# VectorE takes the QK of one head group in turn with softmax and PV of the group before; TensorE sums QK products of four groups

## The chip, the cores and the metric

The kernel runs on one core of a Trainium2 chip. The engines named here are TensorE (PE, its weight loads PEld), VectorE (DVE), ScalarE (ACT), GpSimd (POOL) and SyncE (SP), whose queue issues almost all transfers. The metric is the device time in microseconds (us) of one execution. Kernels are compared by the median over several executions; a profile describes one execution.

## The reference

Input x has 2048 rows of 1024 numbers in bfloat16. Two layers follow, each made of two residual blocks A and B with the same weights in both layers.

```python
def A(x, wqkv, wo):                     # 32 heads of 32, window 8, dilation 2
    q, k, v = split(x @ wqkv)
    idx = pos[:, None] - 2 * arange(8)  # row p sees p, p-2, ... p-14
    mask = idx >= 0
    logits = einsum("bhsd,bhswd->bhsw", q, k[idx]) * 32 ** -0.5
    logits = where(mask, logits, -1e9)
    attn = softmax(logits)
    return einsum("bhsw,bhswd->bhsd", attn, v[idx]) @ wo

def B(x, w1, b1, w2, b2):               # mixes over the rows
    u = gelu(einsum("bsd,sf->bdf", layernorm(x), w1) + b1)
    return transpose(einsum("bdf,fs->bds", u, w2) + b2)

for _ in range(2):
    x = x + A(layernorm(x))
    x = x + B(layernorm(x))
```

## The kernel before

Since the dilation is 2, even and odd rows never meet in A. The kernel calls them the two classes (c = 0 and 1). Within a class, a partition holds J = 8 consecutive rows, so that the window of 8 is reached by slot offsets along the free dimension; the 7 slots ahead of a partition's own rows are copied from the partition before by two transfers (L272 and L273, the shift of k and v). A class has four head groups of eight heads (256 columns), so a layer's attention walks through NCH = 8 chunks, called groups 0 to 7 here: 0 to 3 are class 0, 4 to 7 are class 1.

For one group, `proj` makes q, k or v: per unit 16 matmuls of 256 columns, and one eviction by ScalarE. q, k and v have two buffers each, used alternately by group. `qk` multiplies q with shifted k for two window positions at once (L282, 4096 columns into T4) and folds the 32 products per head to 4 by three halving additions (L283 to L285), four times. `softmax_front` does the last two foldings, adds the mask, takes the maximum by three halving steps and subtracts it; ScalarE takes the exponential. `softmax_back` sums, inverts and normalises into Pb. `pv` multiplies v with Pb (L315). For the groups in `pe_pv` (0 to 3 of layer 0) TensorE adds the eight products up with an identity matrix as weights, and ScalarE copies the sums to o_q; for all others VectorE adds (L340, L343, L344). T4 is the work tile of both `qk` and `pv`. o_q, one buffer, is then transposed by a transfer into oT (L348).

After attention of a class, `out_proj` applies wo, adds the residual, stores the result and normalises it into h2, with statistics on ScalarE for class 0 (`stats_act`) and on VectorE for class 1. `gemm1` is the first product of B. Its sum over the rows needs both classes; for ten of the 14 blocks of w1 the class 0 half is computed ahead (`partials`). `gemm2_tile` is the second product, one tile of 128 rows at a time.

The order is that of the program text, which a planner turns into one in-order instruction stream per engine: it takes the instructions whose inputs are ready, those that stand earlier in the text first. `weave` makes that text: it walks through the units of `stream` (the attention), each with a cost for TensorE and one for VectorE, and whenever TensorE's sum is behind it puts in units of a filler. The filler is first `second_class` (in layer 0 the prologue of class 1, in layer 1 `gemm2_tile` for class 1 of the layer before), then `out_proj` of class 0 and `partials`. The stream's "second" puts in all that is left of the first filler; "out" changes to the next.

In `stream`, the QK units of group ci are followed by units of the projections of group ci+1; after the first QK unit comes `softmax_back` of group ci-1, after the second its whole `pv`. In layer 1 (`split`), softmax and PV of group 3 are done before "second" and before any projection of class 1.

Small tiles of 128x1024 (xr, xn, xs, xo, hb, junk, tmp) share the pool x2 with five buffers.

## Time and profile before

| what | value |
|---|---|
| median of 4 runs | 1376.67 us (1374.45 to 1377.76) |
| profiled execution | 1380.81 us, span 1379.0 us |
| mean granted TensorE clock | 0.979 |
| attention stage of layer 0 | to about 371 us |
| attention stage of layer 1 | about 624 to 1039 us |
| QK products L282 (64 of 4096 columns) | 146.4 us busy |
| PV products L315 (48 of 4096, 32 of 2048 columns) | 148.1 us busy |
| QK foldings L283, L284, L285 | 78.2, 44.1, 27.1 us busy |
| PV additions L340, L343, L344 | 14.7, 44.1, 44.1 us busy |

The span reaches from the first to the last instruction of the profiled execution; 1.8 us of its time lie around it. A line of a group of instructions names the source line, the engine, the operation, what it writes and reads by the program's names, the shape and the count; then the busy time, the mean duration of one in ns, and the idle time of the engine just before them with what ended it. A line of the timeline has the start, the duration, the engine and the group, and in brackets the idle time before it with its releaser. Matmuls overlap, so a mean of 379 ns for a 512-column matmul is a latency; the rate is read from a run of many.

### The profile page before, as it was taken

What the parts mean: (1) busy time and instruction counts of PE and PEld (TensorE: products, weight loads), DVE (VectorE), ACT (ScalarE), POOL (GpSimd) and SP (SyncE); (2) the same over time, 40 slices, a digit from 0 to 9 for tenths busy, and PEclk for the clock granted to TensorE, in tenths of its full rate; (3) what the DMA queues carried; (4) which work ended last, traced back from release to release, by engine and by line L of the source; (5) the groups of instructions that cost most, each with busy time, mean ns of one, the idle gap of its engine ahead of it and who ended that gap; (6) DMA issues with size and microseconds to landing.
All of it is one profiled execution on the core that took longest, in us unless ns stands there. A gap on an engine that the chain in (4) does not pass through costs nothing.

```text
span 1379.0 us, 17728 instructions
## 1 busy us (share of the span) xinstructions
PE 1286.8 (93%) x7328; PEld 742.8 (54%) x7328; DVE 811.1 (59%) x920; ACT 426.5 (31%) x868; POOL 10.5 (1%) x20
## 2 busy tenths in 40 slices
PE   4799889999899999999999979998998999999998
PEld 3677665664344444448866339865443444444443
DVE  4679999999750342233999975966997023211111
ACT  4852228633121341002233433664321234100000
POOL 3000000000000000000000000000000000000000
PEclk9899999999999999999999989999999999999999
DMA  9963334634362326883477883436226322243531
GB/s 221 199 149 89 81 88 135 180 106 106 92 175 61 92 67 174 226 218 87 117 175 188 213 208 102 130 108 151 77 77 180 102 78 69 82 129 101 152 100 58
DMA packets 297985, 177.22 MB, mean 129 GB/s; under 512 B 74704, under 2 KB 275408, under 8 KB 297904
## 3 DMA queue, kind: packets, MB, share of 16 engines
q1 hardware_dynamic: 297792, 176.08, 48.8%
q8 instruction: 57, 0.93, 0.3%
q0 software_dynamic: 112, 0.01, 0.1%
q14 instruction: 24, 0.20, 0.0%
HBM read 127.94 MB, written 16.78 MB: 105 GB/s over the span
## 4 chain that ended last, share of the span: by engine, by line
PE 50%; DVE 37%; DMA 5%; ACT 4%; issue 2%; SPq 1%; DVEq 0%; ACTq 0%
PE psg L476 11%; PE pso L476 11%; PE psg L454 8%; DVE T L282 8%; DVE T L315 7%; PE ps L267 5%; PE pso L454 5%; DVE T L283 4%; PE pso L421 4%; PE ps L454 3%; DVE T L343 3%; DVE o_q L344 3%; DVE T L284 2%; DMA oT<-o_q 2%; DVE St L285 1%
## 5 line engine op out<-in xcount | busy, mean ns | idle before, releaser
L267 PE MATMUL ps<-wq,hT 128*128 128x256 bf16 x3072 | 360.3, 278 | 48.7 <-DMA wq<-in_A_wqkv_dram 27.9
L267 PEld LDWEIGHTS <-hT 128*128 128x128 bf16 x3072 | 325.8, 122 | 88.0 <-issue 28.7
L476 PEld LDWEIGHTS <-w 128*128 128x128 bf16 x1792 | 175.0, 98 | 214.1 <-DMA w<-in_B_w_dram 5.6
L454 PEld LDWEIGHTS <-w 128*128 128x128 bf16 x1792 | 175.3, 98 | 209.7 <-issue 0.8
L454 PE MATMUL psg<-h,w 128*128 128x512 bf16 x896 | 209.9, 379 | 0.2 <-DVE h L216 0.2
L476 PE MATMUL pso<-g,w 128*128 128x512 bf16 x896 | 199.7, 379 | 3.8 <-DMA w<-in_B_w_dram 3.8
L476 PE MATMUL psg<-g,w 128*128 128x512 bf16 x896 | 198.9, 379 | 0.0
L282 DVE TENSOR_TENSOR T<-q,k 128x4096 bf16<-128x4096 bf16 x64 | 146.4, 2288 | 75.3 <-ACT q L269 48.8
L315 DVE TENSOR_TENSOR T<-v,Pb 128x4096 bf16<-128x4096 bf16 (+1 forms) x80 | 148.1, 1864 | 13.0 <-PE psg L330 11.3
L454 PE MATMUL pso<-h,w 128*128 128x512 bf16 x640 | 151.4, 379 | 0.6 <-ACT h L221 0.6
L421 PE MATMUL pso<-wo,oT 128*128 128x512 bf16 x512 | 122.7, 391 | 23.9 <-DMA oT<-o_q 23.2
L465 DVE TENSOR_TENSOR tmp<-pso,g 128x512 f32<-128x512 f32 x40 | 27.7, 692 | 138.0 <-PE pso L454 138.0
L421 PEld LDWEIGHTS <-oT 128*128 128x128 bf16 x512 | 51.0, 100 | 89.3 <-DMA oT<-o_q 24.9
L481 DVE SCALAR_TENSOR_TENSOR xo<-pso,b_sb,xs 128x512 bf16<-128x512 f32 x32 | 23.9, 747 | 119.6 <-PE pso L476 90.2
L481 DVE SCALAR_TENSOR_TENSOR xo<-psg,b_sb,xs 128x512 bf16<-128x512 f32 x32 | 24.0, 750 | 114.5 <-PE psg L476 114.5
L466 ACT ACTIVATE g<-tmp,b_sb 128x512 bf16<-128x512 f32 x80 | 57.7, 722 | 82.1 <-DVE tmp L465 82.1
L283 DVE TENSOR_TENSOR T<-T 128x2048 bf16<-128x2048 bf16 x64 | 78.2, 1222 | 1.2
L269 ACT ACTIVATE v<-ps 128x512 bf16<-128x512 f32 x64 | 37.1, 598 | 96.8 <-DVE T L315 49.0
L181 ACT ACTIVATE ln<-mv,eps 128x1 f32<-128x1 f32 x32 | 9.4, 294 | 179.5 <-DVE mv L190 179.5
L454 PE MATMUL ps<-h,w 128*128 128x512 bf16 x256 | 58.7, 379 | 0.0
L269 ACT ACTIVATE k<-ps 128x512 bf16<-128x512 f32 x64 | 37.5, 592 | 68.2 <-PE ps L267 62.0
L269 ACT ACTIVATE q<-ps 128x512 bf16<-128x512 f32 x64 | 37.8, 592 | 54.7 <-PE ps L267 54.6
(76 smaller groups left out, 752.2 us busy)
## 6 DMA issues: line engine op xcount, KB each, us to landing
w<-in_B_w_dram SPq DMA_DIRECT2D x96, 448.0 KB, 5.0
w<-in_B_w_dram SPq DMA_DIRECT2D x56, 512.0 KB, 4.9
wq<-in_A_wqkv_dram SPq DMA_DIRECT2D x48, 512.0 KB, 4.9
wo<-in_A_wo_dram SPq DMA_DIRECT2D x64, 128.0 KB, 2.9
xa<-xn SPq DMA_DIRECT2D x32, 256.0 KB, 2.1
xs<-xa SPq DMA_DIRECT2D x32, 256.0 KB, 4.7
k<-k SPq DMA_DIRECT2D x16, 392.0 KB, 5.5
v<-v SPq DMA_DIRECT2D x16, 392.0 KB, 5.6
```

The lines of the kernel that those rows point to most:

```text
L267: nc.tensor.matmul(ps[:, jj, :], lhsT=self.lhs(c, kt, j), rhs=wts[part][:, kt, :], start=(kt == 0), stop=(kt == KD - 1))
L269: nc.scalar.activation(out=buf[:, off + 2 * jp:off + 2 * jp + 2, :].rearrange("p j (d h) -> p j d h", h=HQ), in_=ps[:].rearrange("p j (h d ...
L282: nc.vector.tensor_tensor(out=flat, in0=qb, in1=windows(k, u0, WB, [(1, J * QW)]), op=ALU.mult)
L283: nc.vector.tensor_tensor(out=pr[:, :, 0:16, :], in0=pr[:, :, 0:16, :], in1=pr[:, :, 16:32, :], op=ALU.add)
L315: nc.vector.tensor_tensor(out=dst.rearrange("p u j (d h) -> p u j d h", h=HQ), in0=v, in1=pw, op=ALU.mult)
L343: nc.vector.tensor_tensor(out=tf[:, 0], in0=tf[:, 0], in1=tf[:, 1], op=ALU.add)
L344: nc.vector.tensor_tensor(out=of, in0=of, in1=tf[:, 0], op=ALU.add)
L421: nc.tensor.matmul(ps[:], lhsT=at_.oT[c][kt // 2][:, j, kt % 2, :], rhs=wo_t[n][kt // 4][:, kt % 4, :], start=(kt == 0), stop=(kt == KD - ...
L454: nc.tensor.matmul(ps[:], lhsT=wt[c][:, j, fl * P:(fl + 1) * P], rhs=h2[c][:, j, dc * 512:(dc + 1) * 512], start=(k == 0), stop=(k == nk - 1))
L466: nc.scalar.activation(out=gs, in_=tmp[:], func=ACT.Gelu_apprx_tanh, bias=b1_sb[:, ft:ft + 1])
L476: nc.tensor.matmul(ps[:], lhsT=w2t[ft // HF][:, ft % HF, c::DIL], rhs=g[ft // GF][:, ft % GF, dc * 512:(dc + 1) * 512], start=(ft == 0), s ...
L481: nc.vector.scalar_tensor_tensor(out=xo[:, dc * 512:(dc + 1) * 512], in0=ps[:], scalar=b2_sb[:, i, c:c + 1], in1=xs[:, dc * 512:(dc + 1) * ...
```

## The change

- The stream is arranged anew. In the stage of group ci the units of three lists are merged in proportion (`paced`): the QK operations of group ci; softmax and PV of group ci-1, one VectorE operation per unit; and the projections K and Q of group ci+1 followed by V of group ci. V is thus made one stage later than before.
- For the groups in `pe_qk` (0 to 3 of layer 0, the argument that was `pe_pv`), VectorE makes only the products for one window position at a time (2048 columns, two halves of T4 in turn), and TensorE adds eight slices of 256 columns of each with the identity matrix; ScalarE copies the sums of two positions to St.
- PV is done on VectorE, one window position at a time, with a tile of its own (Tv) and additions into o_q, for all groups but the last of each layer; that one (`pv_pe`) is done in two halves of the rows with sums on TensorE, and each half is transposed by its own transfer.
- Maximum and sum of the softmax are one reduction each. The mask is put in by a select on GpSimd, on the first partition, instead of an addition.
- In layer 1, V of group 3 is made after "second", and softmax and PV of group 3 are merged with K and Q of group 4. The unit "even" sets VectorE's sum to no less than TensorE's.
- "out" comes at group 5 in layer 0 (it came within group 4). The pool x2 has four buffers; ScalarE's statistics use h or xs as scratch, and the normalised tile is written over xs.

```diff
-    x2p = pool("x2p", 5)
+    x2p = pool("x2p", 4)
...
-    maskq = const.tile([P, W, J, HQ], BF16, name="maskq")
...
+    Tv = pers.tile([P, J, QW], BF16, name="Tv")
...
         def qk(self, ci):
             q, k = q_t[ci % 2], k_t[ci % 2]
+            if ci in self.pe_qk:
+                for u in range(0, W, WB):
+                    ps = ps_fill(u // 2)
+                    for n in range(WB):
+                        pr = T4[:, n]
+                        nc.vector.tensor_tensor(out=pr, in0=q[:], in1=k[:, u + n:u + n + J, :], op=ALU.mult)
+                        prd = pr.rearrange("p j (g e h) -> p j g (e h)", h=HQ, e=4)
+                        ng = DH // 4
+                        for gi in range(ng):
+                            nc.tensor.matmul(ps[:, n * 256:(n + 1) * 256], lhsT=ident[:], rhs=prd[:, :, gi, :],
+                                             start=(gi == 0), stop=(gi == ng - 1))
+                        if n == WB - 1:
+                            nc.scalar.copy(out=St[:, u:u + WB].rearrange("p u j e h -> p (u j e h)"), in_=ps[:])
+                        yield 0.9, 1.22
+                        yield 0.0, 0.0
+                return
...
+        def softmax(self):
+            Sv = St[:].rearrange("p u j d h -> p (u j) d h")
+            Lu = L[:].rearrange("p u x -> p x u")
             nc.vector.tensor_tensor(out=Sv[:, :, 0:2, :], in0=Sv[:, :, 0:2, :], in1=Sv[:, :, 2:4, :], op=ALU.add)
+            yield 0.0, 0.63
             nc.vector.tensor_tensor(out=L[:].rearrange("p u (j h) -> p (u j) h", h=HQ),
                                     in0=Sv[:, :, 0, :], in1=Sv[:, :, 1, :], op=ALU.add)
+            nc.gpsimd.affine_select(out=L[0:1], in_=L[0:1], compare_op=ALU.is_ge, fill=NEG, base=1 - W,
+                                    pattern=[[1, W], [1, J], [0, HQ]], channel_multiplier=0)
+            yield 0.0, 0.63
+            nc.vector.tensor_reduce(out=m2[:, 0, :], in_=Lu, axis=mybir.AxisListType.X, op=ALU.max)
+            yield 0.0, 0.63
+            nc.vector.tensor_tensor(out=L[:], in0=L[:], in1=m2[:, 0:1, :].to_broadcast([P, W, J * HQ]), op=ALU.subtract)
             nc.scalar.activation(out=L[:], in_=L[:], func=ACT.Exp, scale=scale)
+            yield 0.0, 0.63
+            nc.vector.tensor_reduce(out=m2[:, 0, :], in_=Lu, axis=mybir.AxisListType.X, op=ALU.add)
...
         def pv(self, ci):
+            for u in range(W):
+                dst = Tv if u else o_q
+                v = v_t[ci % 2][:, u:u + J, :].rearrange("p j (d h) -> p j d h", h=HQ)
+                pw = Pb[:, u].unsqueeze(2).to_broadcast([P, J, DH, HQ])
+                nc.vector.tensor_tensor(out=dst[:].rearrange("p j (d h) -> p j d h", h=HQ), in0=v, in1=pw, op=ALU.mult)
+                yield 0.0, 1.16
+                if u:
+                    nc.vector.tensor_tensor(out=o_q[:], in0=o_q[:], in1=Tv[:], op=ALU.add)
+                    yield 0.0, 1.16
+            self.transpose(ci, 0, J)
+
+        def pv_pe(self, ci):
+            hj = J // 2
+            for j0 in (0, hj):
+                accs = [ps_fill(n) for n in range(2)]
+                for u in range(W):
...
+                    nc.vector.tensor_tensor(out=t.rearrange("p j (d h) -> p j d h", h=HQ), in0=v, in1=pw, op=ALU.mult)
+                    tf = t.rearrange("p j c -> p (j c)")
+                    for n in range(2):
+                        nc.tensor.matmul(accs[n][:], lhsT=ident[:], rhs=tf[:, n * 512:(n + 1) * 512],
+                                         start=(u == 0), stop=(u == W - 1))
+                    yield 0.45, 1.3
...
+                self.transpose(ci, j0, hj)
...
+        def paced(self, *its):
+            lists = [it for it in its if it[1]]
+            total = [n for _, n in lists]
+            done = [0] * len(lists)
+            live = [iter(it) for it, _ in lists]
+            while True:
+                k = min((i for i in range(len(lists)) if live[i] is not None),
+                        key=lambda i: ((done[i] + 0.5) / total[i], i), default=None)
+                if k is None:
+                    return
+                u = next(live[k], None)
+                if u is None:
+                    live[k] = None
+                    continue
+                done[k] += 1
+                yield u
...
         def stream(self):
...
-            yield from self.proj(0, 2)
+            yield "even"
+            back = ()
             for ci in range(NCH):
+                last = ci + 1 == NCH
+                turn = self.split and not last and chunks[ci + 1][0] != chunks[ci][0]
                 if self.first and ci == 1:
                     yield "second"
+                if self.first and ci == NQ + 1:
+                    yield "out"
+                parts = [] if last or turn else [self.proj(ci + 1, 1), self.proj(ci + 1, 0)]
+                if not turn:
+                    parts.append(self.proj(ci, 2))
+                yield from self.paced((self.qk(ci), 4 * W // WB), *back, (chain(*parts), len(parts) * J // 2))
+                back = [(chain(self.softmax(), self.pv(ci)), 2 * W + 6)]
+                if turn:
+                    yield "second"
+                    yield from self.proj(ci, 2)
+                    yield from self.paced(*back, (chain(self.proj(ci + 1, 1), self.proj(ci + 1, 0)), J))
+                    back = ()
+                    yield "even"
+                    yield "out"
+            yield from self.softmax()
+            yield from self.pv_pe(NCH - 1)
...
     def gemm2_tile(c, i, w2t, src, dst, hT, on_act=False):
...
-        hb = x2("hb")
         if on_act:
-            nm, rs = stats_act(xo[:], 1.0, eps1)
-            norm_act(hb[:], xo[:], nm, rs)
+            nm, rs = stats_act(xo[:], 1.0, eps1, xs[:])
+            norm_act(xs[:], xo[:], nm, rs)
...
+            if unit == "even":
+                t[1] = max(t)
+                continue
...
                     prologue_tile(1, i, hT)
-                    yield 0.6, 0.0
+                    yield 0.0, 0.0
```

## The prediction

> **What bounds the kernel now.** I read the page's busy shares and slices first, then the timelines of TensorE and VectorE through the two attention stages, then the waits. Busy shares, the rows PE, DVE and PEclk of the slices (34.5 us each), and the chain's sum:
>
> ```profile
> PE 1286.8 (93%) x7328; PEld 742.8 (54%) x7328; DVE 811.1 (59%) x920; ACT 426.5 (31%) x868; POOL 10.5 (1%) x20
> ...
> PE   4799889999899999999999979998998999999998
> DVE  4679999999750342233999975966997023211111
> PEclk9899999999999999999999989999999999999999
> ...
> PE 50%; DVE 37%; DMA 5%; ACT 4%; issue 2%; SPq 1%; DVEq 0%; ACTq 0%
> ```
>
> VectorE is full only in two stretches, the attention of layer 0 (to about 371 us) and of layer 1 (624 to 1039); outside them TensorE is gapless. So only those stretches can move, and each ends when TensorE has done all work that may stand before the class 1 output projection. Their length is TensorE's work plus its idle time. TensorE's timeline where it stood longest (start, duration, group, idle before and its releaser):
>
> ```profile
> 42.79 13.59 PE L267 MATMUL ps<-wq,hT 128*128 128x256 bf16 x96 [6.99 <-DMA wq<-in_A_wqkv_dram]
> ...
> 371.00 26.53 PE L421 MATMUL pso<-wo,oT 128*128 128x512 bf16 x110 [6.84 <-DMA oT<-o_q]
> ...
> 690.84 5.07 PE L267 MATMUL ps<-wq,hT 128*128 128x256 bf16 x32 [4.13 <-ACT v L269]
> ...
> 824.50 1.03 PE L421 MATMUL pso<-wo,oT 128*128 128x512 bf16 x2 [7.97 <-DMA oT<-o_q]
> ...
> 921.51 5.32 PE L267 MATMUL ps<-wq,hT 128*128 128x256 bf16 x32 [2.07 <-ACT k L269]
> ...
> 1038.71 25.49 PE L421 MATMUL pso<-wo,oT 128*128 128x512 bf16 x110 [7.38 <-DMA oT<-o_q]
> ```
>
> Work at full rate: 28 matmuls of 512 columns take 6.04 us in the chain (0.216 each), 192 of 256 columns 21.12 us (0.110). Layer 0 from 42.79 to 371.00 is 328.2 us and holds 1408 projection matmuls (154.9), 128 PV sums (27.6), 144 of the class 0 output projection (31.1), 320 partial sums of the first MLP product (69.1), 18 early ones of class 1 (3.9): 286.6, so 41.6 idle or at a low clock. Layer 1 from 624.42 to 1038.71 is 414.3 us: 1536 projections (169.0), 448 of the second MLP product (96.7), 31.1, 69.1, 3.9: 369.8, idle 44.5. This 86 us is what there is to win.
>
> VectorE's timeline shows what an operation costs from start to start:
>
> ```profile
> 99.67 2.29 DVE L282 TENSOR_TENSOR T<-q,k 128x4096 bf16<-128x4096 bf16 x1 [1.11 <-PE psg L330]
> 101.99 1.23 DVE L283 TENSOR_TENSOR T<-T 128x2048 bf16<-128x2048 bf16 x1
> ...
> 109.82 2.29 DVE L282 TENSOR_TENSOR T<-q,k 128x4096 bf16<-128x4096 bf16 x1
> 112.02 0.68 DVE L292 TENSOR_TENSOR L<-St 128x512 f32<-128x512 bf16 x1
> ...
> 843.00 2.29 DVE L282 TENSOR_TENSOR T<-q,k 128x4096 bf16<-128x4096 bf16 x1 [23.56 <-ACT q L269]
> ...
> 942.16 1.23 DVE L340 TENSOR_TENSOR o_q<-T 128x2048 bf16<-128x2048 bf16 x1 [21.58 <-DMA oT<-o_q]
> ```
>
> Followed by an operation that needs its result, a product of 2.29 takes 2.32 from start to start; followed by an independent one 2.20. So a dependent neighbour adds 0.03, an independent one takes 0.09 off. The two long idles are the turn between the classes (no operation ready while K and Q of class 1 are made) and a PV that waited for its transpose.
>
> **The change, VectorE.** QK by VectorE alone is 2.288 + 1.222 + 0.689 + 0.423 = 4.62, four times 18.5 per head group. In layer 0, groups 0 to 3, it becomes eight products of 2048 columns at 1.22 (row of the PV products of that shape): 9.8, minus 8.7 each. Softmax was 0.692 + 3 x 0.688 + 0.422 + 0.287 + 0.221 before the exponential and 0.422 + 0.290 + 0.224 + 0.551 + 0.690 after: 5.86. Now 0.692 + 0.688, maximum, 0.688, sum, 0.551, 0.690. No reduction is in the trace. Nearest are 0.688 for 512 float32 and 0.422 for 256; I take 0.69, with 1.38 as upper end since it steps 256 bytes between elements. Softmax then is 4.69, minus 18.7 over 16 groups (between plus 3 and minus 27). PV on VectorE was 4 x 2.291 + 7 x 1.225 = 17.7, on TensorE 8 x 1.22 = 9.8; now 15 operations of 1.22, 18.3, for seven groups of a layer, and 16 half products of 0.69 (the 1024-column row) for the last, 11.0. Layer 0 busy: from 4 x 34.2 + 4 x 42.1 = 305 to 4 x 9.8 + 4 x 18.5 + 8 x 4.69 + 7 x 18.3 + 11.0 = 290; layer 1 from 337 to 325.
>
> Taken in turn, a group on VectorE alone has 16 QK and 22 other operations: 41.5 busy, 32 independent neighbours (minus 2.9), 6 dependent (plus 0.2): 38.8, where 290.29 to 332.07 in the trace is 41.8. A group with QK sums on TensorE: 32.8 minus 1.4 plus 0.4: 31.8, where it was 36.2 (133.87 to 170.04).
>
> The mask on GpSimd: a memset of 1x1792 takes 1.722 and of 1x56 0.134, by their slope 512 elements are 0.55; the select that makes the identity takes 0.283 for 128 columns, so 1.13 as upper end. One QK operation (0.34 to 2.3) lies between the logits and the maximum and covers it: uncovered 0 to 0.8 per group, I take 0.2, 3 us in all, the in-order VectorE queue behind it waiting too. The Trainium skill, page "SBUF — State Buffer", section "Who interferes with whom", goes against this: a Vector instruction with two SBUF inputs and a GpSimd instruction that reads SBUF block each other whole, so VectorE would stand for each select; no row here shows it, and by it the sum would hold an estimated 9 to 18 us of VectorE time instead of 3.
>
> **TensorE and the queues.** PV sums go (27.6), 256 QK sums of 256 columns come (28.2), and two last groups with PV on TensorE, 2 x 32 x 0.216 = 13.8: work plus 14. The four St evictions of such a group (about 0.6 each, like ACT's other 512-column casts) replace four casts of o_q. V of a group is now made during its own QK, not a group ahead: its buffer is then already free, which removes waits like the 4.13 at 690.84; in return PV may wait for V's shift (two copies, 5.6 us to landing), covered by the softmax and QK operations ahead (about 13 us), not in the last group, where I count 5. The weights' copies stay equal in number and only change order on SP's queue. The last transpose becomes two, each near 4.4 us; the first passes while the second half is computed, and leftover partial sums fill the rest, so the gaps of 6.84 and 7.38 go. x2 has 4 buffers for 2 tiles per step instead of 5 for 3 (on ACT) or 2: between minus 3 and plus 3, taken as 0. The scratch of the statistics, the normalised tile written over xs, the memsets of the mask and the prologue's pacing (0.6 to 0) cost nothing: ACT is 31% busy, GpSimd 10.5 us.
>
> *Layer 0.* QK of group 0 starts at 44.6 as before, that of group 1 at about 65 (K, Q and 64 sums on TensorE). Three groups of 31.8 end at 160; TensorE needs 4 x 21.1 + 28.2 + 3 (low clock at 42.79) = 116, to 159. Group 4: VectorE 38.8, TensorE 21.1, nothing else ready: 17.7 idle. From 199 TensorE has 49.3 of projections, 6.9 of sums and 100.2 of filler, VectorE 3 x 38.8 and a tail of about 25: TensorE is last. Idle: 3 + 1 + 17.7 + 2 for the clock + 5 of small waits = 29. Gain 41.6 - 29 - 7.5 = 5.
>
> On that clock: after 2.07 idle 32 matmuls took 5.32 (3.5 at full rate), after 2.00 at 308.51 none slowed. So the 17.7 in pieces of 2 us may cost 0 to 14; I take 2. The Trainium skill, page "TensorE: Matmul & The Clock Gate", section "Part 1: The HAM clock gate (the "warmup" mystery)", lets the clock fall only after an idle window of about 3.4 us, by which the same pieces would cost nothing; the 5.32 row shows it fall after less.
>
> *Layer 1.* VectorE starts at 641 as before and needs 19.4 for the first QK, three groups of 38.8 and 12 us of MLP evictions: 789. TensorE has 13.8 + 3 x 21.1 + 96.7 and 4 of weight waits: 802. V of group 3 (7.0) then fills half of the 14.5 us that the last MLP tile takes from its last matmul (811.70) to hT (826.18); idle 7.5 and 2 for the clock. PV of group 3 runs under K and Q of class 1, so the 23.56 idle on VectorE shrinks to a few. QK of group 4 starts near 833 instead of 843. After it VectorE needs 19.4 + 3 x 38.8 + 25: 994; TensorE 176 from 830: 1010. Idle left: 4 + 9.5 + 5 small = 18.5. Gain 44.5 - 18.5 - 7 = 19.
>
> Behind each stretch the class 1 output projection took 26.5 and 25.5 for 110 matmuls (23.7); leftover filler closes half of it, 2, and 0 to 6 more go by a gapless first half of layer 1; I take 3. Sum 5 + 19 + 2 + 3 = 29. The profiled execution took 1380.8 (span 1379.0 and 1.8 around it), 4.1 above the median 1376.7 of the runs; so 1352 in a profile like it, 1348 as the median.
>
> **The rivals.** *A, TensorE hides it:* the gain in VectorE is real, but idle of layer 0 stays and layer 1 gives only the turn: 8 to 12, 1366. For it: TensorE has 14 us more work and is 93% busy, and operations of two groups already alternate at places (109.82, 112.02). Against: the ends' and turn's gaps are named waits.
>
> *B, products wait for sums:* QK products use two halves of T4 and wait for TensorE, which works in order behind projection units of 1.75:
>
> ```profile
> 88.36 1.23 DVE L315 TENSOR_TENSOR T<-v,Pb 128x2048 bf16<-128x2048 bf16 x1 [1.38 <-PE psg L330]
> ```
>
> 24 products in groups 1 to 3 at 1.38 are 33 us of layer 0, and the result 1381 if all come. Against: two or three other operations stand between two products, and only 10 of 32 such products waited (11.3 in all).
>
> *C, slower:* the transposes stand late in SP's order. PV starts by writing o_q and waits for the last transpose, 21.6 at 942.16, and now QK queues behind it as well. Places are groups 5 to 7 of both layers, where residual loads share the queue. VectorE's slack (about 15 in each layer) hides most of one each; four stalls cost 86 - 30 = 56, minus 29: 1404. It decides from three.
>
> **How the numbers follow.** Forecast 0.50, A 0.25, B 0.10, C 0.15. Low: idle of only 20 and 8 left in the two stretches gives 14 + 30 + 5 = 49, 1327. High reaches past B: 1385, leaving out most of C. The forecast's own range is 1327 to 1360. A change within 0.2% (2.8 us) is about what can't be told from none; B falls there by half. Faster 0.77, same 0.04, slower 0.19.
>
> **What would show it.** Right: VectorE busy near 785; group period 38 to 39 in the second half of each layer; no idle over 3 us ahead of the class 1 output projections; VectorE idle at the turn under 10; TensorE idle near 18 in layer 0's group 4. Wrong: products of groups 1 to 3 with waits on the sums (B), o_q's first product waiting for oT (C), reductions well over 0.7, or a maximum that waits for GpSimd in each group.

## The result and the profile after

The changed kernel takes 1381.0 us as the median of 54 executions; the kernel before, on the same chips, 1376.9 us (78 executions). The ratio is 1.0028, 95% interval 1.0021 to 1.0036: slower by 0.3%. The forecast was 1348 us, so the sign is wrong and 33 us are missing. The profiled execution took 1383.15 us, span 1381.3.

The page of the changed kernel: busy time of the engines, and TensorE, VectorE and the granted clock in 40 slices of 34.5 us.

```profile
PE 1296.3 (94%) x7520; PEld 761.7 (55%) x7520; DVE 776.2 (56%) x886; ACT 424.5 (31%) x876; POOL 46.5 (3%) x28
...
PE   3799888998999999999999989998899999999998
...
DVE  4279999999550342324999929999862024211111
...
PEclk9899999999999999999999999999999999999999
```

VectorE has lost 35 us of work (811.1 to 776.2; the prediction said near 785), and GpSimd has gained 36 (10.5 to 46.5). TensorE's work by the two rates of the prediction (0.110 us for 256 columns, 0.2157 for 512) is 3072 x 0.110 + 4256 x 0.2157 = 1256 us before and 3328 x 0.110 + 4192 x 0.2157 = 1270 after: plus 14, as forecast. What the span holds beyond that work is 123 us before and 111 after. The forecast needed 80.

TensorE's timeline at seven places in the changed kernel, five of them long waits:

```profile
186.09 14.96 PE L262 MATMUL ps<-wq,hT 128*128 128x256 bf16 x112 [4.07 <-ACT k L264]
...
345.74 0.61 PE L355 MATMUL pso<-T,ident 128*128 128x512 bf16 x1 [5.09 <-DVE T L352]
...
367.77 2.54 PE L452 MATMUL pso<-wo,oT 128*128 128x512 bf16 x11
...
820.63 1.69 PE L262 MATMUL ps<-wq,hT 128*128 128x256 bf16 x7 [3.59 <-DMA hT<-xs]
...
939.34 0.59 PE L485 MATMUL pso<-h,w 128*128 128x512 bf16 x1 [5.13 <-ACT h L216]
...
993.39 0.50 PE L355 MATMUL pso<-T,ident 128*128 128x512 bf16 x1 [3.76 <-DVE T L352]
...
1014.08 2.11 PE L452 MATMUL pso<-wo,oT 128*128 128x512 bf16 x9
```

The gaps of 6.84 and 7.38 ahead of the class 1 output projection (now L452 at 367.77 and 1014.08) are gone, as forecast. In their place TensorE stands 5.09 and 3.76 us earlier, at the first PV sum of the last group, whose product VectorE has not made. Of the 320 matmuls of partial sums that could have stood there, 16 in layer 0 and 80 in layer 1 (3.5 and 17.3 us) come only with or behind the projection. TensorE also stood 5.76 us at 44.40, 4.95 at 150.60 (for a QK product) and 4.03 at 228.07.

VectorE and GpSimd around the softmax of group 4 in layer 0 (one softmax and PV list in turn with QK of the next group):

```profile
216.40 0.69 DVE L311 TENSOR_TENSOR L<-St 128x512 f32<-128x512 bf16 x1
217.00 1.22 DVE L339 TENSOR_TENSOR o_q<-o_q,Tv 128x2048 bf16<-128x2048 bf16 x1
217.21 4.22 POOL L314 TENSOR_SCALAR_AFFINE_SELECT L<-L 1x512 f32<-1x512 f32 x1 [34.62 <-DVE L L311]
...
218.13 1.22 DVE L297 TENSOR_TENSOR T<-T 128x2048 bf16<-128x2048 bf16 x1
...
219.27 1.22 DVE L336 TENSOR_TENSOR Tv<-v,Pb 128x2048 bf16<-128x2048 bf16 x1
...
221.47 1.04 DVE L317 TENSOR_REDUCE m<-L 128x64 f32<-128x512 f32 x1 [0.98 <-POOL L L314]
```

The select of 512 numbers starts at 217.21, right after the logits. Three operations of VectorE with two inputs (217.00 to 220.49) run beside it; the prediction had thought one such operation enough to cover it. It ends at 221.43, 0.94 us after VectorE fell idle. Its length follows what VectorE has in hand. GpSimd's timeline of three other groups:

```profile
706.32 1.95 POOL L314 TENSOR_SCALAR_AFFINE_SELECT L<-L 1x512 f32<-1x512 f32 x1 [40.07 <-DVE L L311]
747.20 3.09 POOL L314 TENSOR_SCALAR_AFFINE_SELECT L<-L 1x512 f32<-1x512 f32 x1 [38.93 <-ACT xs L216]
786.03 1.08 POOL L314 TENSOR_SCALAR_AFFINE_SELECT L<-L 1x512 f32<-1x512 f32 x1 [35.74 <-DVE L L311]
```

1.08, 1.95, 3.09 and 4.22 are the only lengths that occur, up to 0.01: 1.08 for the select itself, and the rest in steps of 0.87, 1.14 and 1.13, about one operation of VectorE each. At 786.03 VectorE was not standing, and the order is reversed:

```profile
785.82 0.75 DVE L512 SCALAR_TENSOR_TENSOR xo<-psg,b_sb,xs 128x512 bf16<-128x512 f32 x1
786.48 1.64 DVE L339 TENSOR_TENSOR o_q<-o_q,Tv 128x2048 bf16<-128x2048 bf16 x1
788.05 1.04 DVE L317 TENSOR_REDUCE m<-L 128x64 f32<-128x512 f32 x1
```

The select began beside an operation that reads psg, a sum of TensorE, and was not held by it. The addition that began 0.45 us after the select took 1.64 us in place of 1.22, and the maximum did not wait. All six kernels that were traced with the select show this (1.63 to 1.65); with fills in its place (below) the same addition behind the same operation takes 1.22. So of these two, the one that starts first holds the other.

What the select costs is in the next two views: the group rows (instructions, then busy us and mean ns of one, then idle time ahead of them), and the waits (total us, times, longest).

```profile
L314 POOL TENSOR_SCALAR_AFFINE_SELECT L<-L 1x512 f32<-1x512 f32 x16 | 37.2, 2322 | 924.8 <-DVE L L311 557.4 <-ACT k L264 328.4 <-ACT xs L216 38.9
L317 DVE TENSOR_REDUCE m<-L 128x64 f32<-128x512 f32 x16 | 16.6, 1038 | 15.8 <-POOL L L314 15.8
L322 DVE TENSOR_REDUCE m<-L 128x64 f32<-128x512 f32 x16 | 16.5, 1031 | 0.8 <-ACT L L320 0.8
```

```profile
ACT L L320 <- DVE L L319: 58.7, 13, 7.9
...
DVE m L317 <- POOL L L314: 15.8, 15, 1.3
```

The maximum waits for GpSimd 15 times, 15.8 us in all; the sixteenth is the one at 786.03. The line above it may matter too: ScalarE, which takes its instructions in order, stands 58.7 us at the exponential (27.8 us before) because VectorE is late, and what TensorE needs from ScalarE queues behind it. The first wait of TensorE above is such a case, and so is the one at 939.34; ScalarE's timeline there:

```profile
184.93 0.63 ACT L320 ACTIVATE L<-L 128x512 f32<-128x512 f32 x1 [5.76 <-DVE L L319]
185.47 0.58 ACT L264 ACTIVATE k<-ps 128x512 bf16<-128x512 f32 x1
...
933.17 0.63 ACT L320 ACTIVATE L<-L 128x512 f32<-128x512 f32 x1 [5.80 <-DVE L L319]
...
938.05 1.24 ACT L216 ACTIVATE h<-xn,bi,rs 128x1024 bf16<-128x1024 bf16 x1
```

The eviction of K at 185.47 stands behind the exponential; TensorE's 4.07 at 186.09 ends with it. The normalised tile h at 938.05, with its statistics, stands behind the exponential at 933.17; TensorE's 5.13 at 939.34 ends with it.

So the first theory: the select is paid whole, about 1 us a group, on the in-order queue of VectorE, and again through ScalarE's queue. Against it stood: the group sums on TensorE (VectorE now depends on TensorE), the crowded start, the last group's PV, the order of the two lists, the smaller pool, and the reductions, 0.35 us each above what was taken.

### The profile page after: what moved, and what is told of

Its sections match the earlier page's. It is cut to its first block, busy times and chain, and to the rows that moved or that the text cites. A ratio compares the mean times of both kernels' runs of the same rounds, so it can differ in the third digit from the quotient of the medians.

```text
span 1381.3 us, 18146 instructions
## 1 busy us (share of the span) xinstructions
PE 1296.3 (94%) x7520; PEld 761.7 (55%) x7520; DVE 776.2 (56%) x886; ACT 424.5 (31%) x876; POOL 46.5 (3%) x28
## 5 line engine op out<-in xcount | busy, mean ns | idle before, releaser
L507 PEld LDWEIGHTS <-w 128*128 128x128 bf16 x1792 | 174.6, 98 | 215.6 <-DMA w<-in_B_w_dram 8.9
L507 PE MATMUL pso<-g,w 128*128 128x512 bf16 x896 | 200.4, 379 | 5.2 <-DMA w<-in_B_w_dram 5.2
L507 PE MATMUL psg<-g,w 128*128 128x512 bf16 x896 | 199.1, 379 | 0.0
L452 PE MATMUL pso<-wo,oT 128*128 128x512 bf16 x512 | 119.2, 385 | 6.4 <-DMA oT<-o_q 6.4
L295 DVE TENSOR_TENSOR T<-q,k 128x4096 bf16<-128x4096 bf16 x48 | 109.8, 2288 | 21.6 <-ACT q L264 21.1
L339 DVE TENSOR_TENSOR o_q<-o_q,Tv 128x2048 bf16<-128x2048 bf16 x98 | 120.0, 1224 | 0.8
L336 DVE TENSOR_TENSOR Tv<-v,Pb 128x2048 bf16<-128x2048 bf16 x98 | 119.6, 1220 | 0.8
L452 PEld LDWEIGHTS <-oT 128*128 128x128 bf16 x512 | 50.4, 99 | 66.5 <-DMA oT<-o_q 6.9
L314 POOL TENSOR_SCALAR_AFFINE_SELECT L<-L 1x512 f32<-1x512 f32 x16 | 37.2, 2322 | 924.8 <-DVE L L311 557.4
L297 DVE TENSOR_TENSOR T<-T 128x2048 bf16<-128x2048 bf16 x48 | 58.5, 1220 | 0.3
```

The source lines that it names most:

```text
L295: nc.vector.tensor_tensor(out=flat, in0=qb, in1=windows(k, u0, WB, [(1, J * QW)]), op=ALU.mult)
L297: nc.vector.tensor_tensor(out=pr[:, :, 0:16, :], in0=pr[:, :, 0:16, :], in1=pr[:, :, 16:32, :], op=ALU.add)
L314: nc.gpsimd.affine_select(out=L[0:1], in_=L[0:1], compare_op=ALU.is_ge, fill=NEG, base=1 - W, pattern=[[1, W], [1, J], [0, HQ]], channel_m ...
L336: nc.vector.tensor_tensor(out=dst[:].rearrange("p j (d h) -> p j d h", h=HQ), in0=v, in1=pw, op=ALU.mult)
L339: nc.vector.tensor_tensor(out=o_q[:], in0=o_q[:], in1=Tv[:], op=ALU.add)
L452: nc.tensor.matmul(ps[:], lhsT=at_.oT[c][kt // 2][:, j, kt % 2, :], rhs=wo_t[n][kt // 4][:, kt % 4, :], start=(kt == 0), stop=(kt == KD - ...
```

## The experiments

Each time is a median of 4 to 12 executions, with the ratio to the kernel before on the same chip. Where two such ratios have intervals of 0.19% either way, their difference is good to about 0.27%, which is 3.7 us. The differences in us below are those of the medians; taken from the ratios they come out up to 1.7 us larger or smaller.

**The last group's PV on VectorE.**

```diff
-            yield from self.pv_pe(NCH - 1)
+            yield from self.pv(NCH - 1)
```

> The last group of each layer does PV on VectorE alone, like the others, instead of half products summed by TensorE. Theory A (TensorE's work plus its waits is the length of a stage): 64 matmuls of 512 columns go (13.8 us) and with them the waits of 5.09 and 3.76 us for the first half product; the wait for the transpose that comes instead is partly covered by the partial sums that are left over after the stream. 1364 to 1374 us, 7 to 17 below the changed kernel. Rival (VectorE's tail sets the end): 7.3 us more on VectorE per layer and one late transpose: 1381 to 1395 us.

1377.8 us, ratio 1.0006 (0.999 to 1.0022): between the two. TensorE is spared 13.8 us of sums, and the waits for the last transpose are back:

```profile
370.37 1.89 PE L452 MATMUL pso<-wo,oT 128*128 128x512 bf16 x4 [7.97 <-DMA oT<-o_q]
...
1015.10 3.17 PE L452 MATMUL pso<-wo,oT 128*128 128x512 bf16 x7 [6.49 <-DMA oT<-o_q]
```

That part of the change trades about even, and is not where the 33 us are.

**The mask by fills.** The seven masked pieces of row 0 are written by GpSimd, which no longer reads them.

```diff
-            nc.gpsimd.affine_select(out=L[0:1], in_=L[0:1], compare_op=ALU.is_ge, fill=NEG, base=1 - W,
-                                    pattern=[[1, W], [1, J], [0, HQ]], channel_multiplier=0)
+            Lm = L[0:1].rearrange("p u (j h) -> p u j h", h=HQ)
+            for u in range(W - 1):
+                nc.gpsimd.memset(Lm[:, u, 0:W - 1 - u, :], NEG)
```

> The mask is written into the logits by seven small memsets on GpSimd, which read nothing, instead of one select that reads them. Theory B (the select gets no read of the on-chip memory while VectorE runs operations with two inputs, so it runs only once VectorE stands still for it): the maximum's wait for GpSimd falls from 15.8 us to under 4 in all, no GpSimd operation takes over 0.3 us, the exponential's wait on ScalarE falls from 58.7 to under 48 us, and the time by 3 to 10 us, to 1371 to 1378. Rival (any trip over GpSimd costs about 1 us): the wait stays above 10 us and the time at 1379 to 1383.

1365.3 us, ratio 0.9921 (0.9903 to 0.994): 15.7 us less than the changed kernel, more than expected, and faster than the kernel before. TensorE's instruction order is the same in both, so the planner's order is no rival here. The same place in this kernel's timeline:

```profile
214.39 1.21 DVE L340 TENSOR_TENSOR o_q<-o_q,Tv 128x2048 bf16<-128x2048 bf16 x1
214.59 0.47 POOL L316 MEMSET L<- 1x56 f32 x7 [35.06 <-DVE L L311]
215.53 1.22 DVE L297 TENSOR_TENSOR T<-T 128x2048 bf16<-128x2048 bf16 x1
216.66 1.21 DVE L337 TENSOR_TENSOR Tv<-v,Pb 128x2048 bf16<-128x2048 bf16 x1
217.80 1.00 DVE L318 TENSOR_REDUCE m<-L 128x64 f32<-128x512 f32 x1
```

Seven fills take 0.47 us beside a VectorE operation with two inputs, and the maximum doesn't wait. Its wait for GpSimd falls from 15.8 to 2.4 us in all, ScalarE's at the exponential from 58.7 to 45.6, TensorE's 4.07 for K to 2.01.

```profile
ACT L L321 <- DVE L L320: 45.6, 13, 5.8
...
DVE m L318 <- POOL L L316: 2.4, 4, 0.6
```

**Class 1's row statistics of the prologue on VectorE,** to relieve ScalarE at the start.

```diff
-        if c:
+        if False:
```

> The class 1 statistics and normalisation of layer 0's prologue run on VectorE instead of ScalarE. Theory C (in group 0 the evictions of the QK sums and of K queue behind these statistics on ScalarE, which is 20.0 of 20 us busy from 40 to 60): VectorE's 11.0 us wait for St at 68.8 falls under 3, QK of group 1 starts near 66 us instead of 76, and layer 0 ends 4 to 8 us earlier: 1373 to 1377 us. Rival (weights and TensorE bound the start anyway): QK of group 1 starts earlier but TensorE's idle only moves to groups 1 to 4: 1379 to 1383 us.

1387.0 us, ratio 1.0077 (1.0059 to 1.0094): both theories miss. It settles nothing, since the planner also gave TensorE another order: it put 13 sums of group 0 ahead of the next projections, and TensorE waited for them at once. These projections came at 53.81, behind a weight transfer that was issued at 48.88; in the changed kernel they came at 44.40.

```profile
48.69 2.93 PE L284 MATMUL pso<-T,ident 128*128 128x256 bf16 x13 [7.77 <-DVE T L280]
```

**No QK sums on TensorE.**

```diff
-        at_ = Attn(hT, (0, 1, 2, 3) if first else (), first)
+        at_ = Attn(hT, (), first)
```

> No group's QK is summed by TensorE; VectorE folds the products of all groups as in layer 1. TensorE loses 256 matmuls (28.2 us of work), VectorE gains 35 us in layer 0. Theory A with VectorE in groups 1 to 4 as the bound: groups 1 to 3 take 39 to 41 us instead of 32 to 34, TensorE's idle grows there by more than the work that is gone, and layer 0 ends 0 to 8 us later: 1381 to 1389 us. Rival (TensorE's work alone decides): 15 to 25 us less, 1356 to 1366 us.

1416.5 us, ratio 1.0296 (1.0274 to 1.0319): worse than either. With VectorE later still, TensorE's waits for K grow, to 12.6 us at one place:

```profile
PE ps L262 <- ACT k L264: 52.0, 10, 12.6
```

The sums on TensorE, 28 us of its time, save 35. They are not the fault.

**The select twice.** The second changes no value.

```diff
             nc.gpsimd.affine_select(out=L[0:1], in_=L[0:1], compare_op=ALU.is_ge, fill=NEG, base=1 - W,
                                     pattern=[[1, W], [1, J], [0, HQ]], channel_multiplier=0)
+            nc.gpsimd.affine_select(out=L[0:1], in_=L[0:1], compare_op=ALU.is_ge, fill=NEG, base=1 - W,
+                                    pattern=[[1, W], [1, J], [0, HQ]], channel_multiplier=0)
```

> The changed kernel with the GpSimd select of row 0 issued twice in a row for each of the 16 groups; the second changes no value. Writing the seven masked pieces with GpSimd fills instead took 15.7 us off the changed kernel (1381.0 to 1365.3). Theory A (the select stands on VectorE's path whole, about 1 us a group, and what waits behind VectorE in ScalarE's queue is added): the second select costs as much again, 13 to 20 us, so 1394 to 1401 us, and the wait of the maximum for the select goes from 15.8 us to about 32. Rival B (the price is the hand-over between the two engines, and the select's own run time adds little): under 5 us more, 1380 to 1386 us.

1398.0 us, ratio 1.0156 (1.0137 to 1.0174): 17 us more, theory A. The maximum's wait is 31.7 us, 15.9 more. One timeline shows both conditions of the same instruction:

```profile
219.85 1.21 DVE L341 TENSOR_TENSOR o_q<-o_q,Tv 128x2048 bf16<-128x2048 bf16 x1
220.06 4.23 POOL L314 TENSOR_SCALAR_AFFINE_SELECT L<-L 1x512 f32<-1x512 f32 x1 [34.62 <-DVE L L311]
...
220.99 1.21 DVE L297 TENSOR_TENSOR T<-T 128x2048 bf16<-128x2048 bf16 x1
...
222.12 1.21 DVE L338 TENSOR_TENSOR Tv<-v,Pb 128x2048 bf16<-128x2048 bf16 x1
...
224.36 1.08 POOL L316 TENSOR_SCALAR_AFFINE_SELECT L<-L 1x512 f32<-1x512 f32 x1
225.47 1.03 DVE L319 TENSOR_REDUCE m<-L 128x64 f32<-128x512 f32 x1 [2.14 <-POOL L L316]
```

The first select, beside three VectorE operations, takes 4.23; the second, with VectorE standing, 1.08. VectorE stands 2.14, so both ran in that time: the first ended 0.96 us after VectorE fell idle, so beside the three operations it had done at most 0.12 of its 1.08 us.

```profile
DVE m L319 <- POOL L L316: 31.7, 15, 2.4
```

**The maximum twice,** on the kernel with fills: 16.6 us of VectorE more.

```diff
+            nc.vector.tensor_reduce(out=m2[:, 0, :], in_=Lu, axis=mybir.AxisListType.X, op=ALU.max)
             nc.vector.tensor_reduce(out=m2[:, 0, :], in_=Lu, axis=mybir.AxisListType.X, op=ALU.max)
```

> The kernel with GpSimd fills (1365.3 us), with the reduction for the maximum done twice: 16 more reductions of 1.04 us, 16.6 us more of VectorE inside the attention stages. Theory A (VectorE is late against the plan by which TensorE and ScalarE are ordered, so its time is paid whole or nearly): 10 to 18 us more, 1375 to 1383 us; the 11 us by which the two reductions are dearer than my prediction took would then be 7 to 11 us of the miss. Rival B (VectorE has slack in these stages): under 4 us more, 1364 to 1369 us, and the reductions explain nothing.

1376.5 us, ratio 0.9993 (0.9981 to 1.0006): 11.2 us more, theory A. VectorE is busy 57% of the span, and yet a microsecond added to the attention stages costs 0.67 us of time (11.2 / 16.6, good to about 0.2). The planner also changed TensorE's order a little, at 78 of 7520 places.

**The exponential later in ScalarE's queue,** on the kernel with fills.

```diff
-            nc.scalar.activation(out=L[:], in_=L[:], func=ACT.Exp, scale=scale)
             yield 0.0, 0.63
+            for _ in range(4):
+                yield 0.0, 0.0
+            tc.keep_in_program_order(nc.scalar.activation(out=L[:], in_=L[:], func=ACT.Exp, scale=scale))
+            yield 0.0, 0.0
...
-                back = [(chain(self.softmax(), self.pv(ci)), 2 * W + 6)]
+                back = [(chain(self.softmax(), self.pv(ci)), 2 * W + 11)]
```

> The kernel with GpSimd fills (1365.3 us), with the exponential pinned about one eviction later in ScalarE's queue; the work is the same. In that kernel ScalarE stands 45.6 us at the exponential waiting for VectorE, and TensorE stands 8.6 us for evictions of K. Theory A (the exponential's place in ScalarE's in-order queue keeps evictions from TensorE): the wait at the exponential falls below 25 us, TensorE's waits for K below 4 us, time 1358 to 1363 us. Rival B (VectorE would only wait for the later exponential): the sum's wait for the exponential rises from 2.6 us to 8 or more and the time is 1364 to 1369 us.

1375.4 us, ratio 0.9982 (0.9968 to 0.9997): 10 us more than with fills, beyond both ranges. The wait of ScalarE goes as theory A said, and one of VectorE comes that is worse: at the turn of layer 1 the exponential now stands behind evictions of the next class's K.

```profile
DVE m L326 <- ACT L L324: 20.2, 3, 18.2
...
ACT L L324 <- DVE L L320: 4.6, 2, 2.4
```

TensorE's waits for K only fell from 8.6 to 7.4 us. What the wait at the exponential costs by itself stays open, since this run brought a wait of its own.

**A longer plan ahead of the last softmax,** on the kernel with fills.

```diff
+            yield 0.0, 5.0
             yield from self.softmax()
             yield from self.pv_pe(NCH - 1)
```

> The kernel with GpSimd fills (1365.3 us), with 5 us more of VectorE time entered in the plan ahead of the softmax of the last group of each layer, so that about 24 more matmuls of gemm 1's partial sums are placed in front of the sums for PV (32 and 64 of them are otherwise left over after the second out_proj). Theory A (TensorE waits at the sums for products of VectorE only because the planner counts VectorE too short): its waits of 2.51 and 2.38 us in front of those sums go, time 1359 to 1363 us. Rival B (the products are late for another reason and stay as late, or out_proj of class 1 comes later by as much): 1364 to 1368 us.

1359.9 us, ratio 0.9882 (0.9864 to 0.9901): 5.4 us less, theory A. TensorE has no wait ahead of the PV sums any more in either layer. Ahead of the class 1 projection now stand all 320 partial sums in layer 0 and 264 in layer 1, where it was 304 and 240 with fills; what was left over there was thus 16 and 80, not 32 and 64.

**The mask added on VectorE again,** in the changed kernel: this part undone alone. (The mask tile is kept per row and slot, and read for eight heads.)

```diff
-            nc.gpsimd.affine_select(out=L[0:1], in_=L[0:1], compare_op=ALU.is_ge, fill=NEG, base=1 - W,
-                                    pattern=[[1, W], [1, J], [0, HQ]], channel_multiplier=0)
+            nc.vector.tensor_tensor(out=L[:].rearrange("p u (j h) -> p (u j) h", h=HQ),
+                                    in0=L[:].rearrange("p u (j h) -> p (u j) h", h=HQ),
+                                    in1=maskq[:].rearrange("p u j -> p (u j)").unsqueeze(2).to_broadcast([P, W * J, HQ]), op=ALU.add)
```

> One part of the change undone: the mask of row 0 is added on VectorE for all rows again, as in the kernel before (16 additions; the one of before took 0.688 us), and GpSimd has nothing left in the attention stages. Theory A (the move of the mask to GpSimd cost more than it took off VectorE): the 15.8 us wait goes, 11.0 us of VectorE come back, at the 0.6 to 0.7 that the doubled maximum showed (11.2 us of time for 16.6 us of VectorE) 7 us stay of the 15.7, so 1370 to 1375 us, faster than the changed kernel's 1381 and slower than the 1365 with GpSimd fills. Rival B (the move saved as much as it cost): 1379 to 1384 us.

1368.8 us, ratio 0.9944 (0.9925 to 0.9963), a little under theory A's range.

```profile
L318 DVE TENSOR_TENSOR L<-L,maskq 128x512 f32<-128x512 f32 x16 | 11.0, 684 | 0.2
```

This is the whole sign of the result: with 0.684 us more work on VectorE in each group (16 additions, 11.0 us) the kernel is 12 us faster than with the select, and faster than the kernel before.

**The two lists one after the other,** on the kernel with fills.

```diff
-                yield from self.paced((self.qk(ci), 4 * W // WB), *back, (chain(*parts), len(parts) * J // 2))
+                front = chain(*(it for it, _ in back), self.qk(ci))
+                yield from self.paced((front, 4 * W // WB + sum(n for _, n in back)), (chain(*parts), len(parts) * J // 2))
```

> The kernel with GpSimd fills (1365.3 us), with VectorE's work of a group put one list after the other (all of softmax and PV of group n-1, then all QK operations of group n), still in turn with the projections; the work is the same. Theory A (taking turns is what keeps TensorE's sums and the evictions fed): the QK products of a group come some 20 us later in its period, TensorE waits at the QK sums, 1371 to 1385 us. Rival B (the order of the two lists on VectorE does not matter to TensorE): 1362 to 1369 us.

1371.5 us, ratio 0.9965 (0.9951 to 0.998): 6 us more, the low end of theory A. But the edit changes the order of the program text, and the planner went on taking turns:

```profile
109.73 1.21 DVE L337 TENSOR_TENSOR Tv<-v,Pb 128x2048 bf16<-128x2048 bf16 x1
110.87 1.21 DVE L280 TENSOR_TENSOR T<-q,k 128x2048 bf16<-128x2048 bf16 x1
112.00 1.21 DVE L340 TENSOR_TENSOR o_q<-o_q,Tv 128x2048 bf16<-128x2048 bf16 x1
```

Over the two attention stages VectorE changes between the two lists 339 times, and 343 times in the kernel with fills. So the run shows what this other order costs; what taking turns is worth no run here shows.

**Four buffers in the pool x2 of the kernel before.**

```diff
-    x2p = pool("x2p", 5)
+    x2p = pool("x2p", 4)
```

> The kernel before with one part of the change alone: four buffers in the pool of row tiles in place of five. My prediction put this at 0 plus or minus 3 us. Theory A: 1374 to 1380 us. Rival B (loads of residual rows and outputs then wait for buffers): 1382 to 1390 us, with TensorE or VectorE waiting for the residual rows.

1376.1 us, ratio 0.9993 (0.9974 to 1.0011). The pool is worth nothing that shows; the prediction's 0 was right.

**Group 0's QK sums evicted by VectorE,** on fills with the longer plan.

```diff
-                            nc.scalar.copy(out=St[:, u:u + WB].rearrange("p u j e h -> p (u j e h)"), in_=ps[:])
+                            if ci:
+                                nc.scalar.copy(out=St[:, u:u + WB].rearrange("p u j e h -> p (u j e h)"), in_=ps[:])
+                            else:
+                                nc.vector.tensor_copy(out=St[:, u:u + WB].rearrange("p u j e h -> p (u j e h)"), in_=ps[:])
```

> The kernel with GpSimd fills and the padded plan (1359.9 us), with the four evictions of the first group's QK sums on VectorE in place of ScalarE, whose queue is then full with the row statistics of class 1 (VectorE waits 10.1 us there for the fourth). Theory A (the full queue delays everything behind it): that wait falls under 2 us, the QK products of group 1 start near 68 us in place of 76, and the time is 1354 to 1358 us. Rival B (TensorE's work catches up elsewhere, since later groups wait for the same projections): 1358 to 1362 us.

1359.2 us, ratio 0.9876 (0.985 to 0.9902): rival B. The wait of 10.1 us for the eviction is gone, and QK of group 1 starts at 75.07 all the same, for it now waits for its Q:

```profile
75.07 2.36 DVE L280 TENSOR_TENSOR T<-q,k 128x2048 bf16<-128x2048 bf16 x2 [6.52 <-ACT q L264]
```

**Shorter reductions,** on fills with the longer plan: both reductions take five of the eight positions.

```diff
-            nc.vector.tensor_reduce(out=m2[:, 0, :], in_=Lu, axis=mybir.AxisListType.X, op=ALU.max)
+            nc.vector.tensor_reduce(out=m2[:, 0, :], in_=Lu[:, :, 3:8], axis=mybir.AxisListType.X, op=ALU.max)
...
-            nc.vector.tensor_reduce(out=m2[:, 0, :], in_=Lu, axis=mybir.AxisListType.X, op=ALU.add)
+            nc.vector.tensor_reduce(out=m2[:, 0, :], in_=Lu[:, :, 3:8], axis=mybir.AxisListType.X, op=ALU.add)
```

> The kernel with GpSimd fills and the padded plan (1359.9 us), with both reductions over five of the eight window positions: the maximum and the sum leave three positions out. Each reduction then takes about 0.65 to 0.70 us, the 0.69 that the prediction took, and VectorE has 11 us less to do. Theory A (the reductions are most of what is left of the miss): at 0.3 to 0.7 us of time for each us of VectorE, 3.5 to 7.5 us less, 1352 to 1356.5 us. Rival B (with the select gone VectorE has slack): 1358 to 1361 us, and the rest of the miss stays without a cause.

1356.2 us, ratio 0.9843 (0.9821 to 0.9865). A reduction takes 0.709 and 0.704 us now, 10.5 us of VectorE less in all, and 3.8 us of time go: the low end of theory A, and about as large as what two such ratios can tell apart.

**The halving steps back,** on fills with the longer plan.

```diff
-            nc.vector.tensor_reduce(out=m2[:, 0, :], in_=Lu, axis=mybir.AxisListType.X, op=ALU.max)
+            nc.vector.tensor_tensor(out=m4[:], in0=L[:, 0:4, :], in1=L[:, 4:8, :], op=ALU.max)
+            nc.vector.tensor_tensor(out=m4[:, 0:2, :], in0=m4[:, 0:2, :], in1=m4[:, 2:4, :], op=ALU.max)
+            nc.vector.tensor_tensor(out=m4[:, 0, :], in0=m4[:, 0, :], in1=m4[:, 1, :], op=ALU.max)
...
```

> The kernel with GpSimd fills and the padded plan (1359.9 us), with the three halving steps of the kernel before (0.422, 0.288 and 0.222 us there, 0.93 in all) in place of each reduction (1.03 us). Theory A (only VectorE's time counts): 3 us less of VectorE, 1357.5 to 1359.5 us. Rival B (four more dependent starts a group cost more than they save): 1360 to 1363 us.

1354.4 us, ratio 0.9831 (0.981 to 0.9851), the fastest of all: 5.5 us less than with reductions, more than expected; the two ratios' intervals lie just apart (0.9851 and 0.9864). VectorE's busy time falls by 7.5 us (774.8 to 767.3), more than the 3.4 by which the durations add up to less, since the short steps mostly alternate with independent operations and neighbours overlap. The planner also changed TensorE's order a little, at 74 of 7520 places. ScalarE's wait at the exponential falls from 46.8 to 32.8 us.

**The longer plan with the select kept.**

```diff
+            yield 0.0, 5.0
             yield from self.softmax()
             yield from self.pv_pe(NCH - 1)
```

> The changed kernel (1381.0 us) with the padded plan alone, the select kept. Theory A (the two terms add up): the waits of 5.09 and 3.76 us ahead of the PV sums go or shrink, 5 to 9 us less, 1372 to 1376 us. Rival B (the partial sums moved ahead only push out_proj of class 1 back): 1378 to 1382 us.

1369.9 us, ratio 0.9946 (0.9929 to 0.9962): 11.1 us less than the changed kernel, beyond theory A's range. With fills the same line was worth 5.4, so the two do not add up: 15.7 and 11.1 apart, 21.1 together. Part of the lateness at the PV sums was the select's: with fills alone their waits are 2.51 and 2.38, with the select 5.09 and 3.76.

## Why the prediction was wrong

The table shows where each kernel's time lies. Its mark is the first matmul of B's second product of a layer (L476 before, L507 in the changed kernel): from the start to the one of layer 0, from there to the one of layer 1, and the rest of the span. The forecast's row spreads its gains (5 and 1 of the 2 and 3 behind the stages in layer 0, 19 and 4 in layer 1) over the times before.

| kernel | start to it in layer 0 | from there to it in layer 1 | rest | span | span less TensorE's work |
|---|---|---|---|---|---|
| before | 518.7 | 663.1 | 197.2 | 1379.0 | 123 |
| forecast | 512.7 | 640.1 | 197.2 | 1350 | 80 |
| changed | 523.2 | 660.1 | 198.0 | 1381.3 | 111 |
| with fills | 516.4 | 649.9 | 197.6 | 1363.9 | 94 |
| fills, longer plan | 513.7 | 645.9 | 197.6 | 1357.2 | 87 |
| and halving steps | 512.2 | 642.2 | 197.6 | 1352.0 | 82 |

**The mask (wrong, 15.7 us).** The step "One QK operation (0.34 to 2.3) lies between the logits and the maximum and covers it: uncovered 0 to 0.8 per group, I take 0.2, 3 us in all" failed. The select's own time, 1.08 us with VectorE standing, lay inside the bounds of 0.55 to 1.13; what failed is the cover. In 15 of 16 groups the select ran only once VectorE stood, whatever two-input operations lay between, and was then paid nearly whole: 15.8 us of VectorE. The Trainium skill, page "SBUF — State Buffer", section "Who interferes with whom", says that a Vector instruction with two SBUF inputs contends with a GpSimd instruction that reads SBUF, and not with one that only writes it. The prediction weighed this rule, by which 9 to 18 us of VectorE were to be counted, and did not take it for lack of a row. Both halves are what the traces now show: the select (4.23 against 1.08 us) and the fills (0.47 us beside VectorE).

**What VectorE's time is worth (wrong).** The prediction let TensorE be last in both layers and so counted VectorE's time behind the groups as hidden. By the runs it costs 0.67 (the maximum twice), 0.32 (3.5 us for the mask's 11.0) and 0.36 (3.8 us for 10.5) of itself; the last two rest on differences no larger than the 3.7 us that can be told apart. A wait in it costs about all of itself: 15.7 us of time for a wait that shrank by 13.4, 17 us for one that grew by 15.9. Why a wait costs more than work is not shown. One candidate is ScalarE's queue, for which "ACT is 31% busy" was no cover: the exponential in it waits for VectorE (58.7 us), and evictions and statistics that TensorE needs stand behind. The other is the planner, which orders around work that it counts and may not count this wait: TensorE's order is the same with the select as with fills, but differs from it at 79 and 78 of 7520 places with the mask added and with the maximum twice.

**The reductions (mis-sized).** Taken at 0.69, bounded by 1.38; they took 1.04 and 1.03, more than the halving steps they replaced (0.93). That is 11 us of VectorE. The run with 0.71 us each gave 3.8 us.

**The end of each stage (half right, 11.1 us).** The gaps of 6.84 and 7.38 went. "Leftover partial sums fill the rest" failed: the planner's costs put them behind, and 5.09 and 3.76 us of new waits came. With the select kept, five us more in the plan give 11.1; with fills 5.4.

**The group periods (about right in layer 0).** Between the logits of successive groups lie 31.0 and 34.2 us in groups 1 to 3 (said 31.8) and 40.0 twice in groups 4 to 6 (said 38.8). With fills: 30.4, 33.1, 38.9 and 40.5. In layer 1, where 38 to 39 was said for the second half, the changed kernel has 36.7, 26.5 and 40.6 there and 42.0, 40.9 and 38.8 in the first half.

**The start and the turn (wrong, small).** QK of group 1 was to start at 65 and started at 76.23. The run with the evictions moved showed that nothing hangs on the first wait. At the turn VectorE was to stand under 10 us and stood 14.61, for the shift of V of group 3, which is made later now; QK of group 4 started at 838.19 (said 833, before 843.00).

```profile
824.37 1.23 DVE L336 TENSOR_TENSOR o_q<-v,Pb 128x2048 bf16<-128x2048 bf16 x1 [14.61 <-DMA v<-v]
```

**The rivals.** B gave the right time for the wrong reason: QK products waited for TensorE's sums 3 times, 9.2 us in all, not 33. C did not come: no VectorE operation waits for oT, where 21.6 us stood before. A's 1366 is what the kernel with fills takes, by another way. None had the select as its mechanism; the list of signs that would show the forecast wrong did ("a maximum that waits for GpSimd in each group").

With fills, longer plan and halving steps the two stretches of the table take 512.2 and 642.2 us, where the forecast had 512.7 and 640.1. So three terms, the select, the end of each stage and the reductions, hold 26.6 of the 33 us. That the rest of the forecast is right does not follow from these totals, for errors can cancel in them: TensorE's waits at 150.60 (4.95) and 939.34 (5.13) stand in no term of it. Some 6 us of the 33 (1354.4 against 1348) stay without a cause of their own; four of them are the step from the profiled execution to the median, which for this kernel is nil (1353.86 and 1354.4).

## What to carry to other kernels

An operation moved to an idle engine is free only if the two can run at the same time: look for a row where both work, and if there is none, price the move as if neither could. On the in-order queue of an engine that feeds others, a wait of 1 us a group cost about 16 us here and 0.7 us of work a group 3 to 4, so look for waits first; follow them through the third engine's queue as well. Where a planner orders the engines by estimated costs, a filler left over behind a stage, with a wait ahead of it, says that the estimates are short; here one line in the plan mended it.

## What the runs showed that was not expected

- A GpSimd select made no visible progress through three successive two-input operations of VectorE, which left hardly a gap between them (217.00 to 220.49); it was not held for the length of one alone. Where the select began first, it was the two-input operation that took longer (1.64 us in place of 1.22). GpSimd fills beside the same operations ran unhindered (0.47 us for seven).
- A reduction of 512 float32 to 64 along a strided axis took 1.03 us, of 320 to 64 took 0.71: by these two points an estimated 1.7 ns per element beyond a fixed part of about 0.17 us. Three halving steps were cheaper (0.93).
- 1.04 us of extra work a group, on an engine that is 57% busy, was paid at about two thirds of its length.
